# Sequences and decays laid out step by step with the heads side by side, in a gated attention and mixture-of-experts kernel

## The chip, the cores and the metric

The kernel runs on one core of a Trainium2 chip, as one program. The metric is the device time of one execution in microseconds (us). An execution ends when the last instruction has ended, so the chain of work that ends last sets the time.

## What is computed

The reference has two parts. A complex linear recurrence gives a row of 384 numbers for each of 4 x 768 steps (`batch, n_heads, seq, head_dim` are 4, 8, 768, 48):

```python
mag = np.sqrt(a_re * a_re + a_im * a_im)
scale = np.minimum(mag, 0.999) / (mag + 1e-06)
a_re_n, a_im_n = (a_re * scale, a_im * scale)
for t in range(S):
    S_re, S_im = (ar * S_re - ai * S_im + k_t v_t^T, ar * S_im + ai * S_re)
    y[:, :, t] = q_t S_re
```

Each of the 3072 rows of y then goes to the one of 8 experts whose gate logit is largest. The expert is a pair of matrices, 384 x 1024 and 1024 x 384, with a ReLU between them, and its result is weighted by the gate's probability and by a sigmoid of a second gate.

## The kernel before

**Chunks and groups.** The 3072 steps are cut into 24 chunks of 128 steps, with the steps on the 128 partitions and 8 heads x 48 numbers = 384 numbers behind each other. The chunks form groups of 1, 1, 2, 3, 3, 3, 3, 3, 3 and 2; groups are numbered from 0. The loop over time is replaced by cumulated decays: sums of logarithms and of angles over a chunk, made by matmuls with a triangle.

**Loads.** `load(t, src, i)` fetches one chunk of one of the five sequences a_re, a_im, k, q, v with one DMA, issued from SP on line 316. The sequences lie in memory as batch, head, step, 48 numbers. So a load of 128 x 384 numbers (192 KB) is 128 x 8 pieces of 48 numbers, 192 bytes each. `loads_a(g)` loads a_re and a_im of a whole group (tiles `ar` and `ai`, 3 buffers), `loads_b(i)` loads k, q and v of one chunk (7 buffers each). There are 24 x 5 = 120 such loads. The SP engine issues its transfers in order. Between the loads stand its other transfers: the last row of each chunk's decay (`rcs<-re`, line 472), the angle that a chunk hands to the next (`carry<-ai`, line 526), the finished rows (`xd<-xn`, line 653, rows of 1536 bytes) and, late, the experts' weights (`raw`, line 165, rows of 2048 and of 1536 bytes).

**Preparation of a group** (on ScalarE, called ACT, and VectorE, called DVE):

- `prep_exp(g)` makes logarithms of the decays: on ACT `lnr<-ar`, `t<-lnr`, `sq<-ai`, `t<-sq,b_one`, `t<-lnr,b_eps`; between them on DVE `ai<-ai,t` (L409), `lnr<-lnr,t` (L423) and `l<-lnr,t` (L432). Each step needs the one ahead of it.
- `decay(g)`: for each chunk a matmul `cs<-l,tri_l` (L463), and on ACT `re<-cs` and `ri<-cs`, which scale q and k on DVE (L471, L470). `ratios(g)` turns the collected last rows (`rcs`) with a matmul `cs<-ident,rcs` on line 89, which ACT copies out as `rc` (L488). `cs` has two buffers in PSUM.
- ACT then changes its function set (`ACT_TABLE_LOAD`, L192). `prep_trig(g)` takes arctangents (`ai<-ai`), and `turns` and `phase` sum angles (matmul L516), round them off (L520, L521) and take sines (`trig`). From group 4 on, the last angle of a chunk goes to partition 0 by the DMA `carry<-ai`, and L498 on DVE adds it to the next chunk's first row.

**Main line.** For each chunk, `turn` multiplies k and q with the sines (`kc`, `qc`, L564) and transposes them on TensorE (PE, L89), `score` and `values` are matmuls (L606, L620, L626), `state` carries the state to the next chunk (L591, L586), and `finish` and `gates` write the row and its logits. The steps of preparation and main line are mixed by generators, and a scheduler then sets the order on each engine out of its own estimates of how long each instruction and each transfer takes. After the 24th chunk the experts run: for each one matmuls of 128 x 448 on lines 1128 and 1066, with weights that are split into two parts (L179, L180).

A function `recurrence` computes everything step by step; it is entered only where decays are too small, and is not run on these inputs.

Of the kernel before, what the change touches and what calls it, by code (L numbers as in the profile page):

```python
# [21 lines left out]
P = 128  # L22
# [4 lines left out]
TB = 16  # L27
# [5 lines left out]
def tile_gated_attention_moe(  # L33
# [11 lines left out]
    out: bass.AP,  # L45
):
    nc = tc.nc
    B, H, S, D = q.shape
    NC = S // P
    NT = B * NC  # L50
    HD = H * D
# [34 lines left out]
    def turned(out, in_, p0=0):  # L86

        n = in_.shape[0]
        return nc.tensor.transpose(out=out, in_=in_, identity=ident[p0:p0 + n, p0:p0 + n])  # L89

    def tri(name, val, strict=False, dt=F32):
# [21 lines left out]
        out=sel, in_=sel, pattern=[[0, P]], compare_op=ALU.is_ge, fill=0.0,  # L113
# [5 lines left out]
        out=iota, pattern=[[1, NS], [NS, NP]], base=0, channel_multiplier=0, allow_small_or_imprecise_dtypes=True)  # L119
# [5 lines left out]
    def load_gates():  # L125
# [13 lines left out]
        out=entry[:, :, 0], pattern=[[P, NT]], base=-NONE, channel_multiplier=1, allow_small_or_imprecise_dtypes=True)  # L139
# [107 lines left out]
    def at_once(steps):  # L247

        while True:
            try:  # L250
                next(steps)
            except StopIteration as end:
                return end.value
# [26 lines left out]
    def attention(wctx):  # L280
        with ExitStack() as actx:
# [16 lines left out]
            for i in range(2):  # L298
                pair = []
                for n in "qk":  # L300
                    t = pre.tile([P, H, 2, D], F32, name=f"{n}c{i}")
# [3 lines left out]
            for i in range(2):  # L305
                t = pre.tile([P, HD], F32, name=f"state{i}")
# [5 lines left out]
            nc.vector.memset(op, 0.0)  # L312

            def load(t, src, i):
                b, cc = divmod(i, NC)
                nc.sync.dma_start(
                    out=t.rearrange("p (h d) -> p h d", d=D),
                    in_=src[b, :, cc * P:(cc + 1) * P, :].rearrange("h t d -> t h d"))

            where = [(g, c) for g in range(NGR) for c in range(sizes[g])]  # L320
            G = {}
# [527 lines left out]
            a, b, da, db = prep_exp(0), prep_exp(1), decay(0), decay(1)  # L849
# [97 lines left out]
            for kt in range(KT):  # L947
                for c in range(TAIL[1], NT):
# [3 lines left out]
                    out=xl[:, kt, :], in0=accs[kt][:, :CAP], in1=xh[:, kt, :].bitcast(F32), op=ALU.subtract)  # L952
# [221 lines left out]
    def recurrence():  # L1174
        with ExitStack() as rctx:
            one = rctx.enter_context(tc.tile_pool(name="rone", bufs=1))
            rp = rctx.enter_context(tc.tile_pool(name="rp", bufs=1))
            pp = rctx.enter_context(tc.tile_pool(name="rps", bufs=1, space=PSUM))
            R = B * H
            NQ = P // R  # L1180
            DQ = D // NQ
            fold = one.tile([P, R], F32, name="fold")
            nc.gpsimd.memset(fold, 0.0)
            for g in range(NQ):
                nc.gpsimd.affine_select(
                    out=fold, in_=fold, pattern=[[-1, R]], compare_op=ALU.not_equal, fill=1.0,
                    base=-g * R, channel_multiplier=1)
            sre = one.tile([P, DQ, D], F32, name="sre")
            sim = one.tile([P, DQ, D], F32, name="sim")
            nc.vector.memset(sre, 0.0)  # L1190
            nc.vector.memset(sim, 0.0)
            xrow = xd.rearrange("(b s) (h e) -> b h s e", b=B, h=H)
            with tc.For_i(0, S, TB) as t0:
                tiles = {}
                for name, src in (("q", q), ("k", k), ("ar", a_re), ("ai", a_im)):
                    t = rp.tile([P, TB, DQ], F32, name="r" + name)
                    sv = src.rearrange("b h s (g d) -> g (b h) s d", g=NQ)
                    for g in range(NQ):
                        nc.sync.dma_start(out=t[g * R:(g + 1) * R], in_=sv[g][:, bass.ds(t0, TB), :])
                    tiles[name] = t  # L1200
                vt = rp.tile([P, TB, D], F32, name="rv")
                for g in range(NQ):
                    nc.sync.dma_start(
                        out=vt[g * R:(g + 1) * R], in_=v.rearrange("b h s d -> (b h) s d")[:, bass.ds(t0, TB), :])
                ar, ai = tiles["ar"], tiles["ai"]
                tmp = [rp.tile([P, TB, DQ], F32, name=f"rt{n}") for n in range(3)]
                mag, t1, t2 = tmp
                tt = nc.vector.tensor_tensor
                tt(out=t1, in0=ar, in1=ar, op=ALU.mult)
                tt(out=t2, in0=ai, in1=ai, op=ALU.mult)  # L1210
                tt(out=t1, in0=t1, in1=t2, op=ALU.add)
                nc.scalar.activation(out=mag, in_=t1, func=AF.Sqrt)

                tt(out=t2, in0=mag, in1=mag, op=ALU.mult)
                tt(out=t1, in0=t1, in1=t2, op=ALU.subtract)
                nc.vector.tensor_scalar(out=t2, in0=mag, scalar1=2.0, scalar2=1e-30, op0=ALU.mult, op1=ALU.add)
                nc.vector.reciprocal(out=t2, in_=t2)
                tt(out=t1, in0=t1, in1=t2, op=ALU.mult)
                tt(out=mag, in0=mag, in1=t1, op=ALU.add)
                nc.vector.tensor_scalar(out=t1, in0=mag, scalar1=1e-6, scalar2=None, op0=ALU.add)  # L1220
                nc.vector.reciprocal(out=t1, in_=t1)
                nc.vector.scalar_tensor_tensor(out=t1, in0=mag, scalar=0.999, in1=t1, op0=ALU.min, op1=ALU.mult)
                tt(out=ar, in0=ar, in1=t1, op=ALU.mult)
                tt(out=ai, in0=ai, in1=t1, op=ALU.mult)
                part = rp.tile([P, TB, D], F32, name="part")
                w = [rp.tile([P, DQ, D], F32, name=f"rw{n}") for n in range(4)]
                for t in range(TB):
                    wide = lambda x: x[:, t, :].unsqueeze(2).broadcast_to([P, DQ, D])
                    are, aim = wide(ar), wide(ai)
                    tt(out=w[0], in0=sre, in1=are, op=ALU.mult)  # L1230
                    tt(out=w[1], in0=sim, in1=aim, op=ALU.mult)
                    tt(out=w[2], in0=sim, in1=are, op=ALU.mult)
                    tt(out=w[3], in0=sre, in1=aim, op=ALU.mult)
                    tt(out=w[0], in0=w[0], in1=w[1], op=ALU.subtract)
                    tt(out=sim, in0=w[2], in1=w[3], op=ALU.add)
                    tt(out=w[1], in0=wide(tiles["k"]), in1=vt[:, t, :].unsqueeze(1).broadcast_to([P, DQ, D]), op=ALU.mult)
                    tt(out=sre, in0=w[0], in1=w[1], op=ALU.add)
                    tt(out=w[2], in0=sre, in1=wide(tiles["q"]), op=ALU.mult)
                    nc.vector.tensor_reduce(
                        out=part[:, t, :], in_=w[2].rearrange("p d e -> p e d"), axis=AX.X, op=ALU.add)  # L1240
                yt = rp.tile([R, TB, D], F32, name="yt")
                half = TB // 2
                for n in range(2):
                    yp = pp.tile([P, 512], F32, name=f"yp{n}")
                    nc.tensor.matmul(
                        yp[:R, :half * D], fold, part[:, n * half:(n + 1) * half, :].rearrange("p t e -> p (t e)"),
                        start=True, stop=True)
                    nc.vector.tensor_copy(
                        out=yt[:, n * half:(n + 1) * half, :].rearrange("p t e -> p (t e)"), in_=yp[:R, :half * D])
                for b in range(B):  # L1250
                    nc.sync.dma_start(out=xrow[b][:, bass.ds(t0, TB), :], in_=yt[b * H:(b + 1) * H])
            bank = lambda: pp.tile([P, 512], F32, name="rt")
            xpad = one.tile([P, H, DP], F32, name="xpad")
            nc.vector.memset(xpad, 0.0)
            for i in range(NT):
                nc.sync.dma_start(out=xpad[:, :, 0:D], in_=xdv[i].rearrange("t (h d) -> t h d", d=D))
                tp = pp.tile([P, 512], F32, name="xtp")
                for j in range(HP):
                    turned(
                        out=tp[:, j * P:(j + 1) * P], in_=xpad[:, 2 * j:2 * j + 2, :].rearrange("p a b -> p (a b)"))  # L1260
                xt = rp.tile([P, HP, P], F32, name="rxt")
                nc.vector.tensor_copy(out=xt.rearrange("p j t -> p (j t)"), in_=tp)
                for _ in gate_logits(rp, bank, xt, i):
                    pass
            for b in range(B):
                dl, oh = at_once(choose(rp, bank, b * NC, NC))
                for _ in weigh(rp, b * NC, NC, dl, oh):
                    pass
# [71 lines left out]
```

## Time and profile before

| | us |
|---|---|
| median of 3 runs | 560.73 (559.92 to 561.4) |
| the profiled execution, its own time | 562.67 |
| its span, first to last instruction | 560.8 |

| engine | busy us | share of the span |
|---|---|---|
| PE (matmul) | 513.6 | 92% |
| DVE | 339.6 | 61% |
| ACT | 321.8 | 57% |
| GpSimd (POOL) | 100.8 | 18% |

The profile's page cuts the span into 40 slices of 14 us and gives each engine's busy share in tenths. The first 20 slices, to about 280 us, are the recurrence's part, and the rest the experts. The timeline lists instructions by time with the engine's idle time before each and the engine whose work ended it. "DMA share" is the mean busy share of the core's 16 DMA engines.

### The profile page before, as it was taken

The page shows a single profiled execution, that of the slowest core. Times are in us where ns is not written, and L with a number is a line of the kernel's source. Part 1 is how long each engine was busy: PE and PEld are TensorE (multiplying, and loading weights), DVE is VectorE, ACT ScalarE, POOL GpSimd, SP SyncE. Part 2 cuts the span into 40 slices and gives each one's busy share as a digit, 9 for nine tenths or more (in the row PEclk, how much of TensorE's full clock was granted, in tenths as well). Part 3 has the DMA queues.
Part 4 walks back from the last instruction along what each step waited for, and adds up shares of the span by engine and source line. Part 5 has one row for each costly group of instructions (what it writes and reads, how often), then busy time and mean ns, then how long its engine had stood idle before and what let it go on. Part 6 is the DMA issues. An engine that isn't in the chain of part 4 may idle for free.

```text
span 560.8 us, 11096 instructions
## 1 busy us (share of the span) xinstructions
PE 513.6 (92%) x4324; PEld 429.5 (77%) x4324; DVE 339.6 (61%) x763; ACT 321.8 (57%) x603; POOL 100.8 (18%) x124
## 2 busy tenths in 40 slices
PE   2799599899999999998799999999999999999990
PEld 0377466676877778786698999999999999999980
DVE  4578679788979989868556472544526263452120
ACT  5687779698878887767324472544536273552210
POOL 3100011102020302212204433122222310110220
PEclk9999799999999999999899999999999999999995
DMA  9999196666755221034504664351716333220110
GB/s 165 166 186 165 43 162 144 126 139 129 153 96 122 60 72 32 30 123 148 161 14 140 188 192 142 127 155 50 254 38 206 106 136 130 86 76 1 37 32 20
DMA packets 149950, 63.80 MB, mean 114 GB/s; under 512 B 129874, under 2 KB 142005, under 8 KB 149888
## 3 DMA queue, kind: packets, MB, share of 16 engines
q1 hardware_dynamic: 145088, 53.63, 41.7%
q0 software_dynamic: 4800, 9.36, 5.3%
q8 instruction: 36, 0.59, 0.5%
q14 instruction: 26, 0.21, 0.2%
HBM read 54.32 MB, written 10.27 MB: 115 GB/s over the span
## 4 chain that ended last, share of the span: by engine, by line
PE 48%; DVE 1%; DMA 1%; another core or an unknown queue 1%; ACT 0%; issue 0%; POOLq 0%; POOL 0%; DVEq 0%
PE up L1128 21%; PE acc L1066 18%; PE acc L1092 2%; PE yp L89 2%; PE xt L89 1%; PE xt L1092 1%; DMA table<-entry,addr 1%; PE sc L927 1%; PE sc L934 1%; PE yp L713 0%; DMA slots<-table 0%; PE st L934 0%; PE st L927 0%; DVE scores L607 0%; DVE w2l L180 0%
## 5 line engine op out<-in xcount | busy, mean ns | idle before, releaser
L1133 DVE SCALAR_TENSOR_TENSOR hl<-up,hh 128x448 fp32r<-128x448 f32 x64 | 39.9, 624 | 86.5 <-ACT hh L1132 86.2
L1132 ACT ACTIVATE hh<-up 128x448 fp32r<-128x448 f32 x64 | 34.9, 545 | 94.2 <-PE up L1128 81.7
L1128 PE MATMUL up<-xh,w1h 128*128 128x448 f32 x192 | 71.5, 372 | 0.0
L1128 PE MATMUL up<-xl,w1h 128*128 128x448 f32 x192 | 70.5, 367 | 0.0
L1128 PE MATMUL up<-xh,w1l 128*128 128x448 f32 x192 | 70.5, 367 | 0.0
L1066 PE MATMUL acc<-hh,w2h 128*128 128x448 f32 x168 | 63.7, 379 | 0.0
L1066 PE MATMUL acc<-hl,w2h 128*128 128x448 f32 x168 | 61.4, 367 | 0.3 <-DVE hl L1133 0.3
L1066 PE MATMUL acc<-hh,w2l 128*128 128x448 f32 x168 | 61.5, 366 | 0.0
L1079 POOL DMA_INDIRECT out_dram<-y,sid x32 | 30.3, 948 | 154.7 <-ACT y L1101 142.4
L606 PE MATMUL sc<-qt,kt 96*128 96x128 f32 x384 | 51.2, 276 | 0.0
L606 PEld LDWEIGHTS sc<-qt,kt 96*128 96x128 f32 x384 | 47.3, 193 | 1.8 <-issue 1.0
L1014 POOL DMA_INDIRECT rows<-xd,sid x32 | 33.7, 1052 | 64.5 <-DVE w1l L180 26.8
L620 PE MATMUL xo<-scores,v 128*48 128x128 f32 x384 | 41.1, 279 | 0.7 <-DVE scores L607 0.4
L180 DVE TENSOR_TENSOR w1l<-raw,w1h 128x512 fp32r<-128x512 f32 x48 | 30.7, 687 | 16.5 <-ACT w1h L179 11.4
L1128 PEld LDWEIGHTS up<-xl,w1h 128*128 128x128 f32 x192 | 36.1, 188 | 3.5 <-DVE xl L1041 0.2
L1128 PEld LDWEIGHTS up<-xh,w1l 128*128 128x128 f32 x192 | 36.1, 188 | 2.9
L1128 PEld LDWEIGHTS up<-xh,w1h 128*128 128x128 f32 x192 | 36.1, 188 | 2.8
L463 PE MATMUL cs<-l,tri_l 128*128 128x384 f32 x48 | 22.8, 575 | 15.3 <-DVE l L432 10.2
L988 POOL DMA_INDIRECT table<-entry,addr x20 | 23.4, 1172 | 74.4 <-DVE addr L984 69.8
L607 DVE TENSOR_TENSOR scores<-sc,mask 128x512 f32<-128x512 f32 x48 | 32.7, 684 | 5.7 <-PE sc L606 4.9
L626 PE MATMUL xo<-qt,state 96*48 96x128 f32 x320 | 35.2, 275 | 0.0
L1066 PEld LDWEIGHTS acc<-hl,w2h 128*128 128x128 f32 x168 | 31.5, 188 | 3.4 <-DVE hl L1133 0.6
(202 smaller groups left out, 1098.8 us busy)
## 6 DMA issues: line engine op xcount, KB each, us to landing
raw<-in_moe_w_dram SPq DMA_DIRECT2D x32, 768.0 KB
ar<-in_a_re_dram SPq DMA_DIRECT2D x24, 192.0 KB
ai<-in_a_im_dram SPq DMA_DIRECT2D x24, 192.0 KB
k<-in_k_dram SPq DMA_DIRECT2D x24, 192.0 KB
q<-in_q_dram SPq DMA_DIRECT2D x24, 192.0 KB
v<-in_v_dram SPq DMA_DIRECT2D x24, 192.0 KB
xd<-xn SPq DMA_DIRECT2D x24, 192.0 KB
rows<-xd,sid POOLq DMA_INDIRECT x32
```

The lines of the kernel that those rows point to most:

```text
L180: nc.vector.tensor_tensor(out=lo[:, s], in0=raw[:, s], in1=hi[:, s].bitcast(F32), op=ALU.subtract)
L606: nc.tensor.matmul(sp[:, j * P:(j + 1) * P], r["kt"][:D2, h, :], r["qt"][:D2, h, :], start=True, stop=True)
L607: nc.vector.tensor_tensor(out=r["s"][:, 4 * hh:4 * hh + 4, :], in0=sp.rearrange("p (h t) -> p h t", t=P), in1=mask.unsqueeze(1).broadcast_ ...
L620: nc.tensor.matmul(op[u * DP:u * DP + D, j * P:(j + 1) * P], vt[c][:, h * D:(h + 1) * D], r["s"][:, h, :], start=True, stop=(cc == 0))
L626: nc.tensor.matmul(op[u * DP:u * DP + D, j * P:(j + 1) * P], xs[:D2, h * D:(h + 1) * D], r["qt"][:D2, h, :], start=False, stop=True)
L988: ins = nc.gpsimd.indirect_dma_start(out=table, out_offset=bass.IndirectOffsetOnAxis(ap=addr[:, c:c + 1], axis=0), in_=entry[:, c, :], in_ ...
L1014: nc.gpsimd.indirect_dma_start(out=rows[e % 2][:n, i, :], out_offset=None, in_=xd[:known], in_offset=bass.IndirectOffsetOnAxis(ap=sid[:n, ...
L1066: nc.tensor.matmul(accs[kt][:, :CAP], w[:, cs], a, start=(ft == 0 and s == 0), stop=(ft == FT - 1 and s == 2))
L1079: ins = nc.gpsimd.indirect_dma_start(out=out, out_offset=bass.IndirectOffsetOnAxis(ap=sid[:n, e, i:i + 1], axis=0), in_=y[:n, :], in_offse ...
L1128: nc.tensor.matmul(up[:, :CAP], w[:, kt, :], x[:, kt, :], start=(m == 0), stop=(m == 3 * KT - 1))
L1132: nc.scalar.activation(out=hh, in_=up[:, :CAP], func=AF.Relu)
L1133: nc.vector.scalar_tensor_tensor(out=hl, in0=up[:, :CAP], scalar=0.0, in1=hh.bitcast(F32), op0=ALU.max, op1=ALU.subtract)
```

## The change

The five sequences now lie in memory as batch, step, head, 48 numbers, so that the 8 heads of a step are 384 numbers behind each other. They are laid out so before the launch, outside of the kernel's time. A load of one chunk is 128 rows of 1536 bytes. The same 120 loads move the same bytes into the same tiles.

```diff
-    B, H, S, D = q.shape
+    B, S, H, D = q.shape
...
             def load(t, src, i):
-                b, cc = divmod(i, NC)
-                nc.sync.dma_start(
-                    out=t.rearrange("p (h d) -> p h d", d=D),
-                    in_=src[b, :, cc * P:(cc + 1) * P, :].rearrange("h t d -> t h d"))
+                nc.sync.dma_start(out=t, in_=src.rearrange("b (c t) h d -> (b c) t (h d)", t=P)[i])
...
-        a = _np.ascontiguousarray(inputs[name])
+        a = _np.asarray(inputs[name])
+
+        a = _np.ascontiguousarray(a if name.startswith("moe") else a.transpose(0, 2, 1, 3))
```

The loads in `recurrence`, which isn't entered, are split into one for each batch to fit the new layout.

No other line changes, but the scheduler takes the new loads for shorter ones and orders the engines anew. Lines after 318 have numbers smaller by 3 in the changed kernel (316 is now 315). Three places follow. The number behind a tile's name is its buffer's, the same in both.

The first is on ACT in the first 16 us, where the preparation of group 2 (`lnr_229`, `t1_230`) meets the decays of chunks 0 and 1 (`re`, `ri`), up to the first change of the function set. Before:

```order
L198 ACTIVATE kt1_151<-scores_199,b_eps_65 128x384
L198 ACTIVATE re_219<-cs_217 128x384
L198 ACTIVATE ri_220<-cs_217 128x384
L198 ACTIVATE re_237<-cs_235 128x384
L198 ACTIVATE ri_238<-cs_235 128x384
L198 ACTIVATE lnr_229<-ar_167 128x768
L198 ACTIVATE t1_230<-lnr_229 128x768
L192 ACT_TABLE_LOAD
```

Now:

```order
L198 ACTIVATE lnr_229<-ar_167 128x768
L198 ACTIVATE kt1_151<-scores_199,b_eps_65 128x384
L198 ACTIVATE t1_230<-lnr_229 128x768
L198 ACTIVATE re_219<-cs_217 128x384
L198 ACTIVATE ri_220<-cs_217 128x384
L417 ACTIVATE sq_231<-ai_168 128x768
L198 ACTIVATE re_237<-cs_235 128x384
L198 ACTIVATE ri_238<-cs_235 128x384
L192 ACT_TABLE_LOAD
```

The two steps of group 2 stand ahead of the decays, and a third (`sq_231`) between them.

The second is on ACT ahead of the fourth change of the function set, where `prep_exp(4)` (`lnr_608`, `t1_609`, `sq_610`, `t2_611`) meets the decays of group 3 (`re`, `ri`), the ratios of group 2 (`rc_112`) and the copies of the main line (`xn`, `ls`, `xt`). Before:

```order
L652 COPY xn_663<-tr_658 128x384
L210 COPY ls_698<-tr_693 128x128
L198 ACTIVATE en_767<-los_761 128x1
L630 COPY xt_716<-xo_153 128x512
L198 ACTIVATE lnr_608<-ar_294 128x1152
L198 ACTIVATE t1_609<-lnr_608 128x1152
L420 ACTIVATE sq_610<-ai_295 128x1152
L198 ACTIVATE t2_611<-sq_610,b_one_67 128x1152
L198 ACTIVATE re_629<-cs_627 128x384
L198 ACTIVATE ri_630<-cs_627 128x384
L488 COPY rc_112<-cs_642 96x16
L198 ACTIVATE t2_611<-lnr_608,b_eps_65 128x1152
```

Now:

```order
L649 COPY xn_663<-tr_658 128x384
L198 ACTIVATE lnr_608<-ar_294 128x1152
L198 ACTIVATE re_629<-cs_627 128x384
L198 ACTIVATE en_767<-los_761 128x1
L198 ACTIVATE ri_630<-cs_627 128x384
L485 COPY rc_112<-cs_642 96x16
L210 COPY ls_698<-tr_693 128x128
L198 ACTIVATE t1_609<-lnr_608 128x1152
L627 COPY xt_716<-xo_153 128x512
L198 ACTIVATE re_722<-cs_720 128x384
L198 ACTIVATE ri_723<-cs_720 128x384
L198 ACTIVATE re_752<-cs_750 128x384
```

`lnr_608` stands three places earlier, directly behind `xn_663`. The first decays and `rc_112` stand ahead of `t1_609` instead of behind the `sq` and `t2` that follow it, and the other decays (`re_722` to `ri_753`) have moved from behind the last `t2_611` to ahead of the first one. The function set changes behind all of these in both orders.

The third is on SP, at the loads that follow group 2 and 3: the small transfers `rcs<-re` stand between the loads. Before:

```order
L472 DMA rcs<-re 8x1x48
L653 DMA xd<-xn 128x384
L472 DMA rcs<-re 8x1x48
L316 DMA k<-in_k_dram 128x8x48
L316 DMA q<-in_q_dram 128x8x48
L316 DMA v<-in_v_dram 128x8x48
L316 DMA ar<-in_a_re_dram 128x8x48 x2
L316 DMA ai<-in_a_im_dram 128x8x48 x2
L316 DMA ar<-in_a_re_dram 128x8x48
L316 DMA ai<-in_a_im_dram 128x8x48
L472 DMA rcs<-re 8x1x48
```

Now:

```order
L315 DMA v<-in_v_dram 128x384
L469 DMA rcs<-re 8x1x48 x2
L315 DMA ar<-in_a_re_dram 128x384 x3
L315 DMA v<-in_v_dram 128x384
L315 DMA ai<-in_a_im_dram 128x384 x3
L315 DMA k<-in_k_dram 128x384
L315 DMA q<-in_q_dram 128x384
L315 DMA k<-in_k_dram 128x384
L315 DMA q<-in_q_dram 128x384 x2
L650 DMA xd<-xn 128x384
L469 DMA rcs<-re 8x1x48 x2
```

A piece is a whole row (`128x384` instead of `128x8x48`). The three `rcs` of group 3 stood on both sides of nine loads, and now stand ahead of twelve; behind the twelve and one `xd` come the first two `rcs` of group 4.

More of the change, by code (lines that the diff above doesn't have):

```diff
@@ L1196, in recurrence @@
                     t = rp.tile([P, TB, DQ], F32, name="r" + name)
-                    sv = src.rearrange("b h s (g d) -> g (b h) s d", g=NQ)
+                    sv = src.rearrange("b s h (g d) -> g b h s d", g=NQ)
                     for g in range(NQ):
-                        nc.sync.dma_start(out=t[g * R:(g + 1) * R], in_=sv[g][:, bass.ds(t0, TB), :])
+                        for b in range(B):
+                            r = g * R + b * H
+                            nc.sync.dma_start(out=t[r:r + H], in_=sv[g, b][:, bass.ds(t0, TB), :])
                     tiles[name] = t
                 vt = rp.tile([P, TB, D], F32, name="rv")
+                vv = v.rearrange("b s h d -> b h s d")
                 for g in range(NQ):
-                    nc.sync.dma_start(
-                        out=vt[g * R:(g + 1) * R], in_=v.rearrange("b h s d -> (b h) s d")[:, bass.ds(t0, TB), :])
+                    for b in range(B):
+                        r = g * R + b * H
+                        nc.sync.dma_start(out=vt[r:r + H], in_=vv[b][:, bass.ds(t0, TB), :])
                 ar, ai = tiles["ar"], tiles["ai"]
```

## The prediction

> **What bounds the kernel now.** I read the page's slices first, then the chain that ended last, then windows, then the timeline of the windows in which PE has room.
>
> ```profile
> PE   2799599899999999998799999999999999999990
> PEclk9999799999999999999899999999999999999995
> DMA  9999196666755221034504664351716333220110
> GB/s 165 166 186 165 43 162 144 126 139 129 153 96 122 60 72 32 30 123 148 161 14 140 188 192 142 127 155 50 254 38 206 106 136 130 86 76 1 37 32 20
> PE 48%; DVE 1%; DMA 1%; another core or an unknown queue 1%; ACT 0%; issue 0%; POOLq 0%; POOL 0%; DVEq 0%
> ```
>
> PE is full from slice 6 to the end but for a few tenths, so it is PE that sets the end: whatever comes before must be won by letting PE start or go on sooner. There is room in slices 1, 2 and 5, and slice 5 has a lower clock too. The DMA engines are full in slices 1 to 4 and nearly idle in slice 5.
>
> ```profile
> core 0: us, PE busy (x) PEld busy (x) DVE busy (x) ACT busy (x) POOL busy (x), PEclk, DMA share, GB/s
> 0.00:14.00 14.00, 3.27 (x4) 1.00 (x4) 5.73 (x16) 7.96 (x15) 5.00 (x27) 1.00 1.12 165
> 14.00:28.00 14.00, 10.01 (x26) 5.04 (x27) 7.20 (x13) 9.16 (x15) 1.53 (x3) 1.00 1.17 166
> 28.00:42.00 14.00, 13.87 (x193) 10.47 (x193) 10.73 (x19) 11.54 (x22) 0.00 (x0) 1.00 1.19 186
> 56.00:70.00 14.00, 8.47 (x64) 5.88 (x60) 9.55 (x18) 11.09 (x15) 0.00 (x0) 0.76 0.18 41
> 360.00:400.00 40.00, 40.00 (x212) 36.57 (x211) 20.07 (x33) 20.28 (x39) 9.66 (x10) 1.00 0.50 164
> ```
>
> PE is busy 3.27 and 10.01 us of the first two stretches of 14, and 8.47 of the fifth. So about 10.7, 4.0 and 5.5 us are free there; no other 14 us before 240 us have as much. In the first ones the DMA engines are over-full (shares of 1.12 to 1.19) and yet move only 165 to 186 GB/s. Among the experts, where rows are 1536 and 2048 bytes long, half of their time moves 164 GB/s: 164 / 0.50 = 328 GB/s when full.
>
> **Part 1: the load itself.** SP's rows show the pace of the loads:
>
> ```profile
> 0.82 0.44 SPq L316 DMA_DIRECT2D ar<-in_a_re_dram  x1
> 10.02 0.99 SPq L316 DMA_DIRECT2D k<-in_k_dram  x1
> 11.05 1.00 SPq L316 DMA_DIRECT2D q<-in_q_dram  x1
> 49.90 0.38 SPq L653 DMA_DIRECT2D xd<-xn  x1
> ```
>
> The first load is issued in 0.44 us, later ones in 1.0, one each 1.03 us: SP is held up by full queues. 128 x 384 x 4 = 196.6 KB in 1.03 us are 191 GB/s, which agrees with the stretch of 186. A transfer of the same bytes in rows of 1536 (`xd`) is issued in 0.38. At 328 GB/s a load takes 196.6 / 328 = 0.60 us. So each of the 120 loads costs the DMA engines 0.43 us less, and SP about 0.6 us less where queues are full. Only what somebody waits for counts:
>
> ```profile
> 3.93 0.52 ACT L198 ACTIVATE scores<-ar 128x384 f32<-128x384 f32 x1 [1.83 <-DMA ar<-in_a_re_dram]
> 4.48 0.52 ACT L198 ACTIVATE scores<-scores 128x384 f32<-128x384 f32 x1
> 5.36 0.56 DVE L409 TENSOR_TENSOR ai<-ai,scores 128x384 f32<-128x384 f32 x1 [3.76 <-DMA ai<-in_a_im_dram]
> ...
> 14.21 0.84 ACT L198 ACTIVATE lnr<-ar 128x768 f32<-128x768 f32 x1
> 15.09 0.84 ACT L198 ACTIVATE t<-lnr 128x768 f32<-128x768 f32 x1
> ```
>
> The first and third row are the waits for loads at the start. From issue to use the first load takes 3.93 - 0.82 = 3.11 us, of which 1.03 is the transfer; now 2.68, and ACT starts at 3.50. Its two steps take 5.00 - 3.93 = 1.07, so DVE starts at 4.57 instead of 5.36: **0.8 us**. The second load, 0.60 behind the first, is there at 4.1 and is not late. ACT then has two steps of group 2 (Ln and Exp of 768 columns) ahead of the decays, where it stood idle, instead of right ahead of the function set; each takes 0.84 us in the last two rows, so up to 1.7 more. I take 0.8, since chunks 0 to 3 keep PE full from 28 us on (13.87 of 14) and may swallow the rest; the ends are 0 and 2.5.
>
> [...]
>
> **Part 2: the order on ACT ahead of group 3.** This is where the free 5.5 us of the fifth stretch lie.
>
> ```profile
> 53.21 0.48 ACT L652 COPY xn<-tr 128x384 f32<-128x384 f32 x1 [0.27 <-PE tr L89]
> 53.81 0.91 PE L463 MATMUL cs<-l,tri_l 128*128 128x384 f32 x2
> 56.92 1.17 ACT L198 ACTIVATE lnr<-ar 128x1152 f32<-128x1152 f32 x1
> 59.32 1.36 DVE L409 TENSOR_TENSOR ai<-ai,t 128x1152 f32<-128x1152 f32 x1 [0.21 <-ACT t L198]
> 60.71 1.16 ACT L420 ACTIVATE sq<-ai 128x1152 f32<-128x1152 f32 x1 [1.43 <-DVE ai L409]
> 61.91 1.25 ACT L198 ACTIVATE t<-sq,b_one 128x1152 f32<-128x1152 f32 x1
> 63.07 0.47 ACT L198 ACTIVATE re<-cs 128x384 f32<-128x384 f32 x1
> 63.97 2.93 PE L463 MATMUL cs<-l,tri_l 128*128 128x384 f32 x4 [5.08 <-ACT rc L488]
> 64.58 1.25 ACT L198 ACTIVATE t<-lnr,b_eps 128x1152 f32<-128x1152 f32 x1 [0.62 <-DVE lnr L423]
> 67.82 1.28 ACT L192 ACT_TABLE_LOAD   x1
> 76.18 1.08 PE L89 MATMUL tr<-ident,kc 128*96 128x128 f32 x8
> ```
>
> PE waits 5.08 us for `rc`, which stands behind all but the last step of group 4's logarithms. Two microseconds of decays of group 3 then follow that last step, from 65.83 to 67.82. Only then the function set changes, and 8.36 us later PE has chunk 4 to transpose. Now `lnr` follows `xn`: 53.21 + 0.48 = 53.69, 3.23 us earlier. From `lnr` to the function set it took 67.82 - 56.92 = 10.90 us. In the new order the steps behind each other are: `lnr` 1.17; `re`, `en`, `ri`, `rc`, `ls`, 1.6 together by rows such as `re` 0.47; `t` 1.16; then `xt` and three decays, 2.0, with DVE's 1.36 beneath; `sq` 1.16; `ri` 0.48; `t` 1.25; DVE's `lnr` 1.36; `t` 1.25. That is 11.4, less some 0.1 at each of about ten joints, at which ACT starts a step before the last has ended (63.07 + 0.47 = 63.54, and its next row starts at 63.44): 10.5. So the function set changes at 64.2 instead of 67.8: **3.6 us**. It needs the first `cs` by 54.9, and PE has its two matmuls done at 54.7 (53.81 for 0.91 us); if PE is late for the second pair, the term falls to 2. If PE also keeps its clock it is more, see the rivals. The same 8.36 us follow. What comes late next is the arctangent of group 3 and the sums of angles behind it, as now.
>
> **Part 3: small transfers behind loads.** The timeline around 104 us, and the waits ended by the tile `carry` (us, times):
>
> ```profile
> 102.04 1.98 SPq L526 DMA_DIRECT2D carry<-ai  x1
> 106.39 0.55 DVE L498 SCALAR_TENSOR_TENSOR ai<-carry,ai 1x384 f32<-1x384 f32 x1 [2.87 <-DMA carry<-ai]
> 107.00 0.91 PE L516 MATMUL cs<-ai,tri_t 128*128 128x384 f32 x2 [2.29 <-DVE ai L498]
> ```
>
> ```profile
> L526 SPq DMA_DIRECT2D carry<-ai x17: 524/568/2482, 92.0 to 240.7; - x17
> ...
>   DMA carry<-ai: 3.6, 2
> ```
>
> At 102 us the issue of a `carry` took 1.98 us, held up by loads ahead of it, DVE stood for 2.87 us and PE for 2.29. Of 17 `carry` this and one other made DVE wait, 3.6 us in all. With loads of 0.60 instead of 1.03 us SP issues it in the median of 0.57 (1.4 less), and two loads ahead of it save another 0.9: the wait would be gone. What PE then finds to wait for is not in the trace, so between 0 and 2.3; I take **1.0**, near the middle.
>
> The experts' part has the same instructions, PE is full in it, and I cost it at nothing: 40.00 of 40 us in its row, and its loads are unchanged.
>
> **Sum.** 0.8 + 3.6 + 1.0 = 5.4 us. The profiled execution took 562.67 us, a span of 560.8 and 1.87 around it; it would take 557.3. The median of the runs shown is 560.73, 1.94 below the profiled one, so the forecast is 560.73 - 5.4 = **555.3**. The ends are 2 (0 + 2 + 0) and about 10 (2.5 + 5 + 2.3): 558.7 and 550.8. About 0.3%, 1.7 us, is what a measurement of this kernel can tell from no change.
>
> **Rivals.**
>
> *The clock stays up (the larger gain).* In the fifth stretch the granted clock is 0.76, and four matmuls of `cs` take 2.93 us there against 2 x 0.91 = 1.82 for two pairs earlier. With PE's gap shorter the clock may stay up: 1.1 for these, and by my estimate as much again for what PE does up to 68 us; with a start that gives 2 instead of 0.8 the gain is 5.4 + 2.2 + 1.2 = 8.8, 551.9. Against it: a gap of some length remains behind the function set's change. [...] Chance 0.2.
>
> *Loads were hidden anyway (no difference).* Beyond the first two loads no long wait on ACT, DVE or PE ends with a load; if the new order only moves PE's gap, because PE and DVE are late in their turn, 0.8 is left: 559.9. Against it speaks that `lnr` had its input long before it ran, its row naming no wait. [...] Chance 0.09.
>
> *Loads run ahead of small transfers (slower).* The scheduler believes loads to be cheap and puts twelve of them and an `xd` ahead of the `rcs` of group 4. SP issues in order, and a load that waits for its buffer (7 for k, q, v, freed by `kc` and `qc`) holds the `rcs` behind it, and with it POOL's copy, PE's turn of it, `rc` and the state. What such a late transfer costs PE is in the row of 107.00: 2.29. Seven groups, 3 to 9, have such a place. From 5.4 / 7 = 0.8 us for each on, the gain is gone; at 1.15, half of that row, it is 8.0 - 5.4 = 2.6 slower, 563.3. Against it: the `rcs` of group 3 moved the other way, ahead of the loads, and the buffers are the same. Chance 0.08.
>
> That the loads don't become rows of 1536 can be left out: the order shows them as 128 x 384 on both sides.
>
> **How the numbers follow.** The forecast has 0.63, and the larger gain 0.2; both are faster. With the likeliest time of 555.3 the range goes from the larger end, 550.8, to 558.9, which takes in the forecast's own small end; the two other rivals and tails are left out. Faster by over 0.3%: 0.63 + 0.2 = 0.83. Within: 0.09. Slower: 0.08.
>
> **What would show it.** Right: DMA share well below 1 in the first four slices; DVE's first `ai<-ai` near 4.6; the fourth change of the function set near 63 to 64; the first transposes of chunk 4 some 4 us earlier than 76.2, and this lead kept to the experts' start; no wait of `carry` over 1 us. Wrong: chunk 4 as late as before (the second rival), or a lead at chunk 4 that is lost to waits for `rc` or `carry` by 280 us (the third).

## The result and the profile after

The changed kernel takes 558.37 us (median of 20 runs, 554.21 to 563.23); the kernel before, beside it, 562.42 (20 runs, 559.48 to 567.21). The ratio is 0.992 with a 95% interval of 0.9893 to 0.9947: 4.5 us less, between 3.0 and 6.0. Ratios and intervals, here and below, leave out the few executions that fell in a slower state (three of the changed kernel's 20; the median of the other 17 is 557.92), so they need not be the quotients of the medians of all runs. The forecast was 5.4 less. The profiled execution took 559.44 us with a span of 557.2; that of before 562.67 and 560.8.

The page of the changed kernel, its slices and the queue of the loads:

```profile
PE   2899899899989999999799999999999999999990
PEclk9799789999999999999799999999999999999995
DMA  8665433625243110034505563452617243310110
GB/s 282 200 219 155 96 90 101 173 85 150 81 87 115 59 45 31 30 129 145 175 0 171 176 214 107 137 159 71 223 38 232 82 142 126 101 62 1 37 35 17
...
q1 hardware_dynamic: 37568, 53.63, 31.1%
```

The window of the first slice; the last two numbers are the DMA engines' share and the GB/s that they moved:

```profile
0.00:14.00 14.00, 3.27 (x4) 1.00 (x4) 7.24 (x19) 10.34 (x19) 5.27 (x28) 1.00 0.87 282
```

The DMA engines are no longer full: slices 1 to 4 read 8, 6, 6 and 5 instead of 9, 9, 9 and 9, and the first moves 282 GB/s at a share of 0.87 instead of 165 at 1.12. PE is busier in slices 2 and 5 (8 and 8 instead of 7 and 5). The clock's row has new dips in slices 2 and 6; the one in slice 5 was there before.

The start, on ACT and DVE:

```profile
3.35 0.52 ACT L198 ACTIVATE scores<-ar 128x384 f32<-128x384 f32 x1 [1.25 <-DMA ar<-in_a_re_dram]
4.46 0.56 DVE L406 TENSOR_TENSOR ai<-ai,scores 128x384 f32<-128x384 f32 x1 [2.86 <-ACT scores L198]
9.12 0.83 ACT L198 ACTIVATE lnr<-ar 128x768 f32<-128x768 f32 x1
13.83 1.28 ACT L192 ACT_TABLE_LOAD   x1
```

DVE starts at 4.46 (before 5.36, forecast 4.57), group 2's `lnr` runs at 9.12 instead of 14.21, and the function set changes at 13.83 instead of 15.95. Group 3, on ACT and PE:

```profile
50.21 0.48 ACT L649 COPY xn<-tr 128x384 f32<-128x384 f32 x1 [0.27 <-PE tr L89]
50.58 1.17 ACT L198 ACTIVATE lnr<-ar 128x1152 f32<-128x1152 f32 x1
59.77 1.25 ACT L198 ACTIVATE t<-lnr,b_eps 128x1152 f32<-128x1152 f32 x1 [1.53 <-DVE lnr L420]
61.05 1.28 ACT L192 ACT_TABLE_LOAD   x1
```
```profile
69.52 1.65 PE L513 MATMUL cs<-ai,tri_t 128*128 128x384 f32 x2
71.11 1.94 PE L89 MATMUL tr<-ident,kc 128*96 128x128 f32 x8
```

From `lnr` to the function set it takes 61.05 - 50.58 = 10.47 us; 10.5 was forecast. But a pair of sums of angles then takes 1.65 us where it took 0.91, and chunk 4's transposes 1.94 instead of 1.08. The windows of the same stretch show why: from 64 to 74 us PE counts as busy throughout, and the granted clock is 0.50.

```profile
62.00:64.00 2.00, 1.21 (x15) 0.81 (x12) 1.35 (x2) 1.99 (x3) 0.00 (x0) 0.98 0.77 73
64.00:66.00 2.00, 2.00 (x4) 0.50 (x2) 0.00 (x0) 1.03 (x2) 0.00 (x0) 0.50 0.78 207
72.00:74.00 2.00, 2.00 (x7) 1.49 (x6) 1.85 (x4) 1.57 (x4) 0.00 (x0) 0.50 0.36 98
74.00:76.00 2.00, 1.84 (x11) 1.13 (x9) 1.78 (x3) 1.66 (x5) 0.00 (x0) 0.96 0.35 98
```

**A ruler.** ACT's `ACT_TABLE_LOAD` rows cut the recurrence into stretches that can be compared between kernels. The first row is at 0.81 in all of them. In this pair of profiles the second to fifth are at 15.95, 33.62, 67.82 and 80.52 before, and at 13.83, 30.62, 61.05 and 76.52 now. The lead is thus 2.1, 3.0, 6.8 and 4.0 us, and 3.7 when the experts' first matmul starts (287.85 and 284.15).

### The profile page after: what moved, and what is told of

Its sections match the earlier page's. It is cut to its first block, busy times and chain, and to the rows that moved or that the text cites. A ratio compares the mean times of both kernels' runs of the same rounds, so it can differ in the third digit from the quotient of the medians.

```text
span 557.2 us, 11096 instructions
## 1 busy us (share of the span) xinstructions
PE 514.8 (92%) x4324; PEld 429.9 (77%) x4324; DVE 339.0 (61%) x763; ACT 321.1 (58%) x603; POOL 100.2 (18%) x124
## 4 chain that ended last, share of the span: by engine, by line
PE 48%; DVE 1%; DMA 1%; another core or an unknown queue 1%; ACT 0%; issue 0%; POOLq 0%; POOL 0%; DVEq 0%
PE up L1125 21%; PE acc L1063 18%; PE acc L1089 2%; PE yp L89 2%; PE xt L89 1%; PE xt L1089 1%; DMA table<-entry,addr 1%; PE sc L924 1%; PE sc L931 1%; DMA slots<-table 0%; PE yp L710 0%; PE st L931 0%; PE st L924 0%; DVE w2l L180 0%; DVE scores L604 0%
## 5 line engine op out<-in xcount | busy, mean ns | idle before, releaser
L180 DVE TENSOR_TENSOR w1l<-raw,w1h 128x512 fp32r<-128x512 f32 x48 | 30.7, 686 | 16.3 <-ACT w1h L179 12.7
L1063 PEld LDWEIGHTS acc<-hh,w2l 128*128 128x128 f32 x168 | 31.6, 188 | 2.3
```

The source lines that it names most:

```text
L180: nc.vector.tensor_tensor(out=lo[:, s], in0=raw[:, s], in1=hi[:, s].bitcast(F32), op=ALU.subtract)
L1063: nc.tensor.matmul(accs[kt][:, :CAP], w[:, cs], a, start=(ft == 0 and s == 0), stop=(ft == FT - 1 and s == 2))
```

## The experiments

My theory after the result was the one of the prediction: the new order on ACT makes most of the gain, the transfers only the earlier first step. The rival: shorter transfers make it, in any order. To part them, each engine's instructions were held in a given order, whatever the scheduler would choose:

```diff
     with _tile.TileContext(nc) as tc:
         tile_gated_attention_moe(tc, *args)
+        follow(tc, ORDER)
...
+def follow(tc, order):
...
+    for row in json.loads(zlib.decompress(base64.b85decode(order))):
...
+        for one, two in zip(row, row[1:]):
+            behind(two, one)
```

`ORDER` holds one list of instructions for each engine, and each must be issued behind the one ahead of it.

### Rows and order apart

**Rows alone**: the changed kernel in before's order.

> The changed layout and loads of 1536-byte rows, but every engine's instructions in the order that before had. Theory (the order on ACT makes the gain, at two places; the transfers themselves give only an earlier first step): DVE's first ai near 4.5 instead of 5.36 and everything behind it about 0.9 us earlier; function sets change at 15.0, 32.7 and 66.9, and the time is 0.9 us under before (0 to 1.5), a ratio of 0.998. Rival (the shorter transfers themselves make the gain, whatever the order): 3.6 to 4.5 us under before, 0.992 to 0.994.

**Order alone**: the kernel before in the changed kernel's order.

> Before's layout and loads of 192-byte rows, but every engine's instructions in the order of the changed kernel. Theory (order makes the gain): at the start group 2's Ln, which stands at 9.12 in the changed kernel, waits for its ar, issued at 7.82 in before and there about 3 us later, so the start gains next to nothing; at group 3 the fourth change of the function set still comes 3.8 us sooner behind xn, of which 2.7 are lost again to the slow clock: 1 to 2 us under before, 0.997 to 0.998. Rival 1 (the transfers make the gain): same as before within 0.3 us or slower. Rival 2 (the order pays only with loads that land early): 1 to 3 us slower than before, with new waits for loads at group 3 too.

**Rows, and one part of the order each**: the lists of before, with one part of the changed kernel's lists put in. For the start these are places 3 to 20 of ACT's list and 5 to 16 of DVE's; for group 3, places 66 to 80 of ACT's, 67 to 102 of DVE's, 219 to 300 of PE's, 28 to 30 of POOL's and 49 to 143 of SP's.

> Loads of 1536-byte rows and before's order, except that on ACT and DVE the instructions ahead of the second change of the function set stand as in the changed kernel. Theory: the whole lead of the start, 3.0 us at chunk 1's kc (25.3 instead of 28.3), and kept to the end since group 3 runs as in before: 3.0 us under before, 0.9947. Rival (the lead of the start is absorbed at group 3, where PE waits for rc): 1 us or less, 0.998.

> Loads of 1536-byte rows and before's order, except that around group 3 (ACT ahead of the fourth change of the function set, and DVE, PE, POOL and SP there) instructions stand as in the changed kernel. Theory: 0.9 us from the first step, 3.8 us at the fourth change of the function set (63.1 instead of 67.8), 2.7 given back by a slow clock up to chunk 5: 2.0 us under before, 0.9964; without the slow clock 4.7. Rival (the transfers make the gain): the same as the kernel with rows alone.

Measured against the same runs of before (median 558.71), with 95% intervals: rows alone 0.9938 (0.9900 to 0.9977), order alone 1.0159 (1.0108 to 1.0211), rows and start 0.9946 (0.9911 to 0.9980), rows and group 3 0.9918 (0.9880 to 0.9956).

So the theory failed in time: rows alone give 3.5 us, as much as times can tell of the whole change, and the order alone loses 8.9. The intervals of the three kernels with wide rows overlap, so times don't rank them. Where the order loses, the rows of ACT and SP show (order alone):

```profile
12.46 0.84 ACT L198 ACTIVATE lnr<-ar 128x768 f32<-128x768 f32 x1 [2.72 <-DMA ar<-in_a_re_dram]
...
66.91 0.49 ACT L198 ACTIVATE re<-cs 128x384 f32<-128x384 f32 x1 [3.27 <-DMA rcs<-re]
```
```profile
60.50 2.62 SPq L316 DMA_DIRECT2D ar<-in_a_re_dram  x3
63.22 0.90 SPq L653 DMA_DIRECT2D xd<-xn  x1
64.29 0.67 SPq L472 DMA_DIRECT2D rcs<-re  x1
65.05 0.40 SPq L316 DMA_DIRECT2D v<-in_v_dram  x1
65.54 2.50 SPq L472 DMA_DIRECT2D rcs<-re  x2
```

Group 2's `lnr`, put early, waits 2.72 us for a narrow load. At group 3 the third `re` may not overwrite its buffer before `rcs<-re` has read it, and SP issues that one behind three loads and an `xd`: ACT stands for 3.27 us. This is the prediction's third rival, and it happens only with narrow rows. The two waits don't make the whole loss. In this profile the stretch behind the second change of the function set is 4 to 6 us longer than in before's two profiles (21.78 in the table below), because matmuls there take almost twice their time up to 35 us (eight transposes 1.94 us instead of 1.08); more on that with the run that has POOL.

### Both kernels once more, for what changes by chance

The profiles compared so far come from two sets of runs, in which before's median was 562.42 and 558.71. So before and after were run once more beside each other, unchanged. Before again has one run only.

> The kernel before, unchanged, for a second profile beside the runs of this set. Theory (some waits of one profile are chance: the clock's rise, and PE's pauses that end with nothing the profile shows): spans and the times of chunk 1's kc differ from the first profile of before by 1 to 3 us, and the pauses called issue or remote (2.3 us on PE in the first) are absent or elsewhere. Rival (they belong to narrow rows): the same pauses of 1.5 to 3 us in the same places.

> The changed kernel, unchanged, on the same chip as the others of this set. Theory: 0.992 of before as measured first (0.989 to 0.995), and in its profile the clock low for several us behind the fourth change of the function set again. Rival (that low clock was chance): clock 1.00 there, and chunk 4's transposes up to 2.7 us sooner.

After again: 554.44 against 558.94, a ratio of 0.9934 (0.9896 to 0.9972). The function sets of after again:

```profile
14.13 1.28 ACT L192 ACT_TABLE_LOAD   x1
31.76 1.28 ACT L192 ACT_TABLE_LOAD   x1
62.20 1.28 ACT L192 ACT_TABLE_LOAD   x1
75.23 1.28 ACT L192 ACT_TABLE_LOAD   x1
```

The same cut made in every profile, us between changes of the function set ("up" is the start of the experts' first matmul):

| kernel | to 2nd | 2nd-3rd | 3rd-4th | 4th-5th | 6th-7th | 11th-12th | 13th-14th | up |
|---|---|---|---|---|---|---|---|---|
| before | 15.95 | 17.67 | 34.20 | 12.70 | 15.48 | 15.77 | 19.73 | 287.85 |
| before again | 15.79 | 15.71 | 34.21 | 12.69 | 17.14 | 15.78 | 19.74 | 283.01 |
| rows alone | 14.99 | 16.02 | 34.21 | 12.69 | 14.65 | 15.78 | 19.73 | 279.63 |
| order alone | 17.18 | 21.78 | 33.79 | 13.62 | 15.82 | 17.57 | 20.17 | 292.05 |
| rows, start | 13.65 | 15.81 | 34.21 | 12.70 | 15.06 | 15.78 | 19.73 | 277.60 |
| rows, group 3 | 15.04 | 17.45 | 30.44 | 12.96 | 14.50 | 15.77 | 19.73 | 277.50 |
| after | 13.83 | 16.79 | 30.43 | 15.47 | 14.83 | 16.65 | 20.17 | 284.15 |
| after again | 14.13 | 17.63 | 30.44 | 13.03 | 14.45 | 16.65 | 20.18 | 276.75 |

Most stretches repeat to 0.03 us, so single profiles can be compared there, though times of one kernel spread over 7 to 10 us and the sets of runs are from different chips. The stretch from the last change of the function set to "up" isn't in the table: it takes from 42.5 to 45.6 us in these eight, with after again and after at the two ends. Five things are read off.

- *To the 2nd change*: 15.9 before, 15.0 with wide rows, 13.7 to 14.1 with the start's order too. Rows give 0.9 and the order 1.2.
- *3rd to 4th*: 34.2 in before's order with either rows, 30.4 in the new order with wide rows, 33.8 with narrow ones. The order gives 3.8 and needs the wide rows for it, or, as a later run shows (30.7 with narrow rows), small transfers that don't stand behind loads.
- *4th to 5th*: 12.7 in before's order, in the new one 13.0 or 15.5 (13.6 in order alone). The new order always pays 0.3 back there and, with a long dip of the clock as in the windows above, 2.8.
- *11th to 12th and 13th to 14th*: 0.9 and 0.4 longer in the new order, in every profile that has its late part (with narrow rows 1.8 and 0.4). "Rows, group 3" has before's late part and doesn't pay. Which instructions cost it wasn't followed.
- *2nd to 3rd* is 15.7 or 17.7 for the same kernel. PE's rows show why, before and before again: the second time the same matmuls take little more than half as long. The windows' granted clock reads 1.00 there in both, so in these two profiles only the matmuls' own times show the slow speed.

```profile
24.03 1.94 PE L89 MATMUL tr<-ident,kc 128*96 128x128 f32 x8
```
```profile
23.12 1.08 PE L89 MATMUL tr<-ident,kc 128*96 128x128 f32 x8 [0.67 <-DVE kc L564]
```

The short pauses of PE, 0.3 to 0.5 us each, that end with nothing the profile shows are chance too, as the expectation for before again said. PE, before, then before again, at the same instructions:

```profile
129.19 0.42 PE L208 MATMUL tr<-xt,wg 128*32 128x128 f32 x3 [0.42 <-issue]
129.93 0.38 PE L208 MATMUL tr<-xt,wg 128*32 128x128 f32 x2 [0.31 <-issue]
```
```profile
127.86 0.39 PE L208 MATMUL tr<-xt,wg 128*32 128x128 f32 x6
```

They add up to 2.3 us in the first profile of before and 1.7 in that of after, and to nothing in both later ones. So the pair of profiles shown first misleads twice: both have such pauses, and that of after has the long dip.

### How much a transfer's own time matters

The load's pieces were made shorter and longer, in before's order:

```diff
-                    out=t.rearrange("p (h d) -> p h d", d=D),
+                    out=t.rearrange("p (h d) -> p h d", d=WL),
...
+            a = a.transpose(0, 2, 1, 3).reshape(b, t, 16, 24).transpose(0, 2, 1, 3)
```

(4 and 96 in place of 16 and 24 for the longer ones.)

> Before's order on every engine, with the sequences laid out so that a load has pieces of 96 bytes (16 to a row) instead of 192. The step-by-step recurrence, which isn't entered, is not adapted to that layout. Theory (the transfers' own time makes the gain, so a longer one must cost): a load takes 2.06 us of the DMA engines instead of 1.03, five loads 10.3 us where a chunk takes about 10.5, so loads are just kept up with; first step 1.5 to 2 us later, SP's small transfers 1 to 3 us later each: 8 to 20 us slower than before, 1.015 to 1.035. Rival (order alone counts and loads are hidden): within 0.5% of before but for the first step's 1 to 2 us.

> Before's order on every engine, sequences laid out so that a load has pieces of 384 bytes (4 to a row). The step-by-step recurrence, which isn't entered, is not adapted to that layout. A load took 1.42 us with pieces of 96 bytes, 1.03 with 192 and 0.60 with 1536, that is 0.4 to 0.5 ns for each piece; 512 pieces give 0.8 us. Theory (the gain follows the load's time): about half of the 3.4 us of whole rows in this order, 1.5 to 2 us under before, 0.997, and carry's waits between those of before and of whole rows. Rival (any row that keeps the engines below full is enough): 3 us or more, 0.994.

With 96 bytes SP issues a load every 1.4 to 1.5 us, and the DMA engines are eight tenths full or more in 13 of the first 14 slices:

```profile
DMA  9999999798898854103450556253343426040010
```

The time is 588.12 us, 1.0527 of before (1.0467 to 1.0586): 29 us slower, more than the 8 to 20 that I expected. ACT waits 6.1 us for group 4's `ar`, and DVE 19.3 us in all for `carry`. With 384 bytes SP issues a load every 0.75 us and the first stretch of 14 us moves 219 GB/s, but the time is 559.66 against 558.35, 1.0021 (0.9970 to 1.0072). The half gain that I expected (0.997) isn't seen, though the interval just reaches it. The 2nd change comes 0.5 us sooner (15.38), the 6th to 7th takes 17.08, about as in before again, and the 2nd to 3rd happened to take 19.36, with pairs of sums of angles at 1.6 us up to 27. So going from 96 to 192 bytes is worth 29 us here, and twice that length bought nothing more that can be measured.

### The small transfers behind the loads

What carries the gain of rows alone beyond the first step? Its "up" is 3.4 us sooner than that of before again: 0.8 from the start and 2.5 from the 6th to 7th stretch. That stretch holds a `carry`, and 1.7 of the 2.5 us are the clock: before itself took 15.48 there, not 17.14. The windows behind the wait for `carry`, before again, then before:

```profile
106.00:108.00 2.00, 2.00 (x11) 1.53 (x10) 0.96 (x2) 0.86 (x2) 0.00 (x0) 0.50 0.81 135
```
```profile
108.00:110.00 2.00, 2.00 (x28) 1.38 (x27) 1.85 (x5) 1.15 (x3) 0.00 (x0) 1.00 0.93 132
```

The clock dips there in before again and in the kernel with 384 bytes (17.14 and 17.08 us for the stretch), and, with the 96-byte kernel left aside, in no other profile. PE's wait behind that `carry` was 2.25 to 2.63 us in four profiles with rows of 192 or 384 bytes, and two of the four dip; it was at most 2.05 us in the nine others, all those with wide rows among them, and none dips. So a shorter wait may also spare a dip, but two against two don't show it. SP and DVE, before again, then after:

```profile
100.08 1.82 SPq L526 DMA_DIRECT2D carry<-ai  x1
```
```profile
104.48 0.55 DVE L498 SCALAR_TENSOR_TENSOR ai<-carry,ai 1x384 f32<-1x384 f32 x1 [3.07 <-DMA carry<-ai]
```
```profile
97.85 0.57 SPq L523 DMA_DIRECT2D carry<-ai  x1
```
```profile
101.76 0.55 DVE L495 SCALAR_TENSOR_TENSOR ai<-carry,ai 1x384 f32<-1x384 f32 x1 [2.23 <-DMA carry<-ai]
```

The issue shrinks from 1.82 to 0.57 us, but the wait doesn't go: 3.9 of 4.4 us from issue to use are left. In three kernels the small transfers were therefore taken out of SP's queue (PE, ACT and DVE keep their order; POOL's is left to the scheduler):

```diff
-                    (nc.gpsimd if g < 2 else nc.sync).dma_start(
+                    ins = nc.gpsimd.dma_start(
                         out=d["rcs"][c * H:(c + 1) * H, :D], in_=re[127:128, :].rearrange("p (h d) -> p h d", d=D))
...
-                    nc.sync.dma_start(out=st["carry"], in_=fr[127:128, :])
+                    ins = nc.gpsimd.dma_start(out=st["carry"], in_=fr[127:128, :])
```

> Loads of 192-byte rows with the changed kernel's order on PE, ACT and DVE, as in the run that was 9 us slower, but the small transfers rcs (from group 2 on) and carry are issued by POOL instead of SP, out of the loads' queue. Theory (with narrow rows the new order loses because small transfers stand behind loads in SP's queue): ACT's third re of group 3, which stood 3.27 us for rcs, waits under 0.5 us; between the second and fourth change of the function set 30.5 us instead of 33.8; carry waits under 2 us in all; 4 to 5 us less than that run, 1.007 to 1.009 of before, what is left being group 2's Ln at the start. Rival (the loads themselves are late): the same waits and 1.016.

> The kernel before (192-byte rows, its order on PE, ACT and DVE), with rcs (from group 2 on) and carry issued by POOL. Theory (part of what the wide rows bring is that small transfers get past the loads): the carry that stood 2.9 and 3.1 us in two profiles of before waits 1 to 2 us, 1 to 2.5 us under before, 0.996 to 0.998. Rival (its own 3 us from issue to landing make the wait, or the full DMA engines): the same wait, within 0.2% of before.

> The changed kernel with its order on PE, ACT and DVE, and rcs (from group 2 on) and carry issued by POOL. Theory (with rows of 1536 bytes the small transfers hardly wait behind loads; what carry still waits is its own way from issue to landing, 3.0 us): the same as the changed kernel within 0.2%, 0.990 to 0.994 of before, DVE's waits for carry 3 to 5 us in all as in three profiles with wide rows. Rival (loads still hold them up): carry waits under 1 us and 1.5 to 3 us under the changed kernel, 0.987 to 0.990.

Against before's 558.35: order alone with POOL 1.0073 (1.0027 to 1.0120), before with POOL 1.0095 (1.0049 to 1.0141), after with POOL 0.9964 (0.9915 to 1.0012). All three pay something that I hadn't thought of. POOL's last row and the span, after again and after with POOL:

```profile
core 0 of [0], span 550.1 us
...
535.49 0.94 POOL L1076 DMA_INDIRECT out_dram<-y,sid  x1 [0.64 <-DVE y L1164]
```
```profile
core 0 of [0], span 552.6 us
...
534.15 0.94 POOL L1079 DMA_INDIRECT out_dram<-y,sid  x1 [0.64 <-DVE y L1167]
```

From the end of this last row to the end of the span it is 550.1 - 536.4 = 13.7 us (13.2 to 13.7 in every kernel without the move), and with 39 more transfers on POOL 552.6 - 535.1 = 17.5, in "before with POOL" as well (561.0 - 543.5). These 3.8 us are 0.7%.

- *Order alone with POOL*: the theory holds where it named a place. ACT's third `re` waits 0.25 us instead of 3.27, and the 3rd to 4th takes 30.74 instead of 33.79. With the 0.7% taken off it is 1.0005 instead of 1.0159; that the time fell where I expected it is luck, since I hadn't seen the 0.7%. Nor is all of the difference the queue's. "Up" comes 6.4 us sooner than for order alone (285.66), and 4.7 of these are in the 2nd to 3rd stretch (17.07 instead of 21.78). PE's rows of the two agree to 0.2 us up to 25 us; then eight transposes take 1.08 us from 27 us on here and from 36 on there. Order alone, then with POOL:

```profile
33.42 1.94 PE L89 MATMUL tr<-ident,kc 128*96 128x128 f32 x8
```
```profile
30.39 1.08 PE L89 MATMUL tr<-ident,kc 128*96 128x128 f32 x8
```

So how much of the 8.9 us belongs to the queue isn't shown; the 3.05 us of the 3rd to 4th are. The 4th to 5th takes 15.48 here, with narrow rows, and 15.47 in after. The `lnr` of the start still waits 2.7 us for its load, and carry's waits didn't fall (5.5 us).

- *Before with POOL*: the 6th to 7th falls from 15.48 (17.14 with the dip) to 13.91, but other `carry` wait now, 9.6 us in all; the 9th to 10th takes 21.41 instead of 19.75 and the 10th to 11th 16.23 instead of 14.90. "Up" is at 283.79, no sooner than before again. My 1 to 2.5 us weren't there.
- *After with POOL*: carry still waits 3.9 us in all, and "up" is at 275.43, 1.3 sooner than after again; the 2nd to 3rd stretch alone, which took 17.67 and 15.71 in before's two profiles, is 1.7 shorter (15.98). In wide rows the queue no longer matters, as expected.

### The slow clock

> The changed kernel with its order kept, and matmuls whose results are overwritten put into PE's waits at three places: 14 ahead of the first sum of angles, 12 and 5 in the waits ahead of group 3's sums of angles, 18 ahead of the last chunk's gate logits. Theory (the slow clock takes back part of the gain): clock 1.00 from 60 to 76, chunk 4's transposes 1.7 to 2.7 us sooner behind the function set's change, chunk 1's kc up to 1.5 sooner, and up to 2 from 272 to 280: 3 to 6 us under the changed kernel, 0.982 to 0.987 of before. Rival (the slow clock is hidden behind ACT and DVE): less than 1 us, 0.990 to 0.992.

```diff
+                        fill = [nc.tensor.matmul(
+                            op[u * DP:u * DP + D, j * P:(j + 1) * P], vt[c][:, h * D:(h + 1) * D], ident,
+                            start=True, stop=True) for _ in range(12 if (i, j, u) == (3, 2, 0) else 0)]
```

(and the same ahead of group 0's and group 3's first sum of angles and the last gate logits.) The profile is of the longest of its 12 executions, 560.05 us, so it is read for the clock and not for the time. PE's rows at the start, and at group 3:

```profile
12.42 4.55 PE L519 MATMUL st<-ident 128*128 128x128 f32 x28
...
22.89 1.64 PE L525 MATMUL cs<-ai,sel 32*128 32x384 f32 x2
```
```profile
63.79 2.67 PE L627 MATMUL xo<-ident,v 128*48 128x128 f32 x23
...
69.34 0.91 PE L525 MATMUL cs<-ai,sel 32*128 32x384 f32 x2
```

At group 3 the clock stays at 1.00 from 58 to 78 us, and a pair takes 0.91. But the filling is longer than the waits were (each filling matmul counts twice in the rows; they take 2.67 us in place of a wait of 1.72), so the 4th to 5th takes 13.29, no better than 13.03 without it. At the start the clock falls to 0.50 at 22 us all the same, although PE had been busy from 12.4 to 20.7 but for 0.8 us, and then waited 0.7. The 2nd to 3rd stretch takes 20.90 there (17.63 in after again) and that from the last change to "up" 46.72 (42.54), so the filling at these two places shows no gain either. The time is 0.9954 of before (0.9914 to 0.9995), not below after's. So the dip explains 2.4 us of one profile of after, but I have no kernel that turns it into a gain.

## Why the prediction was right, and where it was not

**Part 1 (0.8 forecast).** Its first half is close: DVE at 4.46 against 4.57, loads at 282 / 0.87 = 324 GB/s against 328, and the 2nd change 0.9 us sooner from rows alone. The other half failed. I had cut the order's "up to 1.7 more" to nothing, since, as I wrote, chunks 0 to 3 keep PE full and may swallow it. They don't: the 3rd to 4th stretch is as long as before (34.21 us) for a kernel that enters it sooner, so a lead of the start is handed on whole. The term is 2.0.

**Part 2 (3.6 forecast).** The term itself is right: 3.8 us between the 3rd and 4th change, in every profile with that order and wide rows. The step that failed is "the same 8.36 us follow". They were 10.06 in the profile of after and 8.00 in that of after again (62.20 to 70.20), and to the 5th change 2.8 or 0.3 us are given back. What raises and lowers the clock isn't shown. In before PE paused for 5.08 us and the granted clock read 0.50 from 62 to 66 us; in after PE's longest pause just ahead of the dip was 1.72 us, and the clock read 0.50 from 64 to 74 with PE busy throughout. And with nothing changed, before's 2nd to 3rd stretch took 17.67 and 15.71 us.

**Part 3 (1.0 forecast).** The size is near and the reason half. Wide rows shorten the 6th to 7th stretch to 14.45 to 15.06, 14.7 in the mean, from the 15.48 of before: 0.8 us. The 17.14 of before again has a dip of the clock in it, which I hadn't thought of. I wrote that "the wait would be gone", but DVE still waits 4.2 us in all for `carry` (3.6 and 5.0 in before's two profiles), and PE's wait behind that `carry` shrinks from 2.29 to 1.64 us. My own numbers left 2.87 - 1.4 - 0.9 = 0.6 us of DVE's wait. SP's slow issue goes (0.57 us instead of 1.82); most of the way from issue to use stays (3.9 of 4.4 us).

**Costed at nothing.** The experts: right, 255.9 us from the first `up` to the last `acc` in every profile. The order of the recurrence behind group 3: wrong, it costs 1.3 us. I looked for the change of order only where it helped.

**Sum.** 2.0 + 3.8 - 0.3 + 0.8 - 1.3 = 5.0 us with the 4th to 5th stretch of after again (13.03) and 2.5 with that of after (15.47), and 1.7 more against a profile of before with the dip behind `carry`. Measured were 4.5 (3.0 to 6.0) and, the second time, 3.7 (1.6 to 5.8). That the forecast of 5.4 was so close is partly luck: a term too small, a term given back and a cost not seen nearly cancel.

**The rivals.** That the clock stays up didn't happen: in the profile of after it read 0.50 from 64 to 74 us, and in that of after again the 4th to 5th stretch was no shorter than before's either (13.03 against 12.70). That loads are hidden anyway, with 0.8 us left, is refuted by the time itself (3.0 to 6.0 less) and, a little less clearly, by rows alone (1.3 to 5.6 less). That loads run ahead of small transfers is a true mechanism, with 3.27 us for one wait of ACT, but it showed only with narrow rows. What I hadn't seen is that the order and the rows aren't two parts to be added: at group 3 the new order gains only where no small transfer stands behind long loads.

Still open: times alone can't tell rows alone from the whole change (0.9938 and 0.9934), so that the order's net share is positive rests on the stretches of single profiles. They give 1.2 + 3.8 - 0.3 - 1.3 = 3.4 with after again's 4th to 5th stretch, 0.9 with after's. Wide rows with the new order at the start and at group 3 but before's late part should be 1.3 us better than the change; it wasn't run.

## What to carry to other kernels

When a transfer becomes shorter, look for the small transfers that share its queue before the ones that wait for the long one: behind narrow loads one cost ACT 3.27 us here, and 0.25 out of their queue. A scheduler that orders by its own estimates turns a change of data layout into a change of order, so all four combinations have to be tried, since the new order may need the new layout (here 1.0159 without it and 0.9934 with it). Cut profiles at an instruction that all versions have, and compare stretches: most repeated to 0.03 us where whole times spread over 7 to 10. Before a stretch that doesn't repeat is credited to an edit, look at the clock and at the matmuls' own times in it.

## What was not expected of the hardware

- The granted clock stayed at 0.50 for 10 us while PE counted as busy in every one of them (64 to 74 us, sums of angles and transposes), and at 0.50 from 22 to 32 us in a kernel that had kept PE busy from 12.4 to 20.7 but for 0.8 us.
- In two of four profiles in which PE waited 2.25 to 2.63 us for a `carry`, the granted clock fell behind it (0.50 from 106 to 108 us in before again), and the stretch took 1.6 and 1.7 us longer than in before.
- At the start matmuls took up to twice their later time (1.94 against 1.08 us for eight transposes in before's profile, at 24 us) while the granted clock read 1.00; how long this lasted differed by up to 9 us between two profiles with one order (to 36 and to 27 us).
- 39 small transfers moved from SP's queue to POOL's lengthen the end of the program, behind the last instruction in the profile's rows, from 13.7 to 17.5 us.
- Loads in pieces of 384 bytes are issued every 0.75 us instead of 1.03, yet the kernel isn't measurably faster; loads in pieces of 96 bytes every 1.4 to 1.5 us, and it is 29 us slower.
